# Moving four value loads behind a later head's rows, and their casts into the next unit, in a fused clustered-attention and gated feed-forward kernel

## The chip, the cores and the metric

The kernel runs on one core of one Trainium2 chip. The metric is device time in microseconds of one execution; the median of several executions is given. Beside it stands the profile of one execution: its own time, and its span, which is the time from its first to its last profiled instruction.

## The reference

Attention over 4 batches of 8 heads, 768 tokens each, head width 64. Each query and each key is assigned to the nearest of 16 centroids of its head, and a query sees only the keys of its own cluster. The result, as 3072 tokens of 512 features, goes through an RMS norm and a gated feed-forward network with 1536 hidden features.

```python
q_assign = np.argmax(np.einsum('bhsd,hcd->bhsc', q_n, c_n), axis=-1)   # q_n, k_n, c_n: normed
k_assign = np.argmax(np.einsum('bhsd,hcd->bhsc', k_n, c_n), axis=-1)
mask = q_assign[:, :, :, None] == k_assign[:, :, None, :]
scores = np.where(mask, scale * np.matmul(q, k.transpose(0, 1, 3, 2)), -1e9)
attn = softmax(scores)                              # over the keys
x = (attn @ v).transpose(0, 2, 1, 3).reshape(3072, 512)
xn = x / np.sqrt(np.mean(x * x, -1, keepdims=True) + 1e-6) * rms_g
g = xn @ w_gate
out = (g * sigmoid(g) * (xn @ w_val)) @ w_out
```

Inputs and output are float32; the kernel multiplies in bfloat16.

## The kernel before

**Units and groups.** The 32 heads (numbered 0 to 31 over batches and heads) are loaded and prepared in 8 groups of four (`group_work`); group 4 is heads 16 to 19, group 5 heads 20 to 23. The attention itself goes in 8 units, `u` = 0 to 7: unit `u` is half of the queries of batch `u // 2`, over all 8 heads of that batch. So "third unit" is `u` = 2 and "fourth unit" is `u` = 3. Groups 4 and 5 are batch 2 and are first used in the fifth unit, `u` = 4.

**Preparing a head.** SyncE's queue loads its query and key rows (`load`, L84; four transfers of 48 KB for each of the two from head 13 on) and its values (`load_v`, L103; one transfer of 192 KB). VectorE transposes the rows (`trans`, L213; L218 in the profile), GpSimd (POOL) casts them to bfloat16 into `qext` and `kext` (`cast`, L241). GpSimd also casts the values into `vbf` (`vcast`, L244). Cluster products on TensorE (L255) and comparisons on VectorE give a one-hot row of the cluster of each token, and GpSimd's queue places these by DMA under the transposed rows (`place`, L298). `vbf`, `qext` and `kext` have four buffers each, taken by group number modulo 4; the loaded values have eight buffers, and the loaded rows six.

**One unit.** For each head, TensorE computes the scores (L349), ScalarE takes the exponential (L353), and TensorE multiplies with the values one head later (`pv`, L367). Between these stands the work of earlier units: the feed-forward products of the unit before (L447, with the gate's nonlinearity on ScalarE and two products on VectorE, L468 to L473), and the output products of the one before that (L485), copied by ScalarE (L488) and stored by SyncE's queue (L489).

**From attention to feed-forward.** `rms` (L406) norms a unit's rows on VectorE (L412), and, from the second unit on, a DMA transpose issued from SyncE's queue (L417) makes `xnT`, which the gate and value products of L447 read. In the trace this transpose for the second unit's rows stands at the start of the third unit, and so on.

**What sets the order.** It is written by hand: every engine runs its instructions in program order, and the queue of an engine issues its DMAs in program order. `attention` (L690) walks over the heads of a unit and takes pieces of work from the list `fill`, each with a weight in us of TensorE work, so that they spread evenly; pieces of weight 0.0 follow the piece before them at once. In the loop at the end (L711 on) the list for a unit is: the rest of the earlier unit's feed-forward products; `rms`; then loads of query and key rows (the heads in `LATE`, L58); then output products interleaved with the rows of a new group; then feed-forward products interleaved with that group's cluster work. Group 3 is prepared in the second unit, group 4 in the third, group 5 in the fourth.

**The function that the change touches.** In `group_work`, `others(n)` runs once for each head `n` of a group, between its query cast and its key cast: it casts the head's values, loads those of head `n + 4` (`AV` = 4), and loads the rows of head `n + 6`, where these are not in `LATE`. So values of 16 to 19 are loaded during group 3's preparation, and cast during group 4's.

Of the kernel before, what the change touches and what calls it, by code (L numbers as in the profile page):

```python
# [22 lines left out]
def kernel(  # L23
# [21 lines left out]
    HG = 4  # L45
# [11 lines left out]
    AV = 4  # L57
    LATE = {2: (18, 19, 20, 21), 3: (23, 24, 25), 4: (28, 29)}  # L58
# [21 lines left out]
    def src(a, n):  # L80
        b, h = divmod(n, H)
        return a[b, h].rearrange("(p t) d -> p t d", t=ST)

    def load(n, part, on=None):  # L84
        if n not in staged:
            staged[n] = stage.tile([P, 2, ST, D], F32, tag="qk", name="qk")
        if n < BH:
            (on or nc.sync).dma_start(out=staged[n][:, part], in_=src((q, k)[part], n))
            return

        to = staged[n][:, part].rearrange("p t d -> p (t d)").rearrange("p (i r d) -> p i r d", i=HT, d=32)
        of = (q, k)[part][n // H, n % H].rearrange("(r p i e) (c d) -> e c p i r d", p=32, i=HT, e=2, d=32)
        for e in range(2):
            for c in range(2):
                r = 32 * (2 * e + c)
                nc.sync.dma_start(out=to[r:r + 32], in_=of[e, c])

    def load_qk(n):
        if n < B * H:
            load(n, 0)  # L100
            load(n, 1)

    def load_v(n, vq=None):  # L103
        if n >= B * H:
            return
        stagedv[n] = stage.tile([P, ST, D], F32, tag="vs", name="vs", bufs=NV)
        (vq or nc.sync).dma_start(out=stagedv[n], in_=src(v, n))
# [99 lines left out]
    def load_o(c):  # L207
        nc.gpsimd.dma_start(out=wo[:, c:c + 4], in_=moe_w_out[c * P:(c + 4) * P].rearrange("(c p) f -> p c f", p=P))
# [4 lines left out]
    def trans(g, h, part, on=None):  # L213
        if (g, h // 2) not in qkT:
            qkT[g, h // 2] = qk32.tile([P, 2, 2, UQ], F32, tag="qkT", name="qkT")
        qk = staged[g * HG + h]
        if g * HG + h >= BH:
            nc.vector.transpose(qkT[g, h // 2][:, h % 2, part], qk[:, part].rearrange("p t d -> p (t d)"))  # L218
            return
        ps = ps_g.tile([P, UQ], F32, tag="gen", name="tq")  # L220
        for i in range(HT):
            nc.tensor.transpose(ps[:, i * P:(i + 1) * P], qk[:, part, 2 * i:2 * i + 2].rearrange("p t d -> p (t d)"),  # L222
                                ident_f)
        to, by = qkT[g, h // 2][:, h % 2, part], 1.0 / ZS if part and g < BG else 1.0
        if on is nc.vector:
            nc.vector.tensor_scalar_mul(to, ps, by)  # L226
        else:
            nc.scalar.activation(to, ps, ACT.Copy, scale=by)  # L228
# [5 lines left out]
    def cast(on, g, h, part, es=(0, 1)):  # L234
        for e in es:
            to = cols((kext if part else qext)[g % 4][:D, h], g, e)
            of = qkT[g, h // 2][e * D:(e + 1) * D, h % 2, part]
            if on is nc.scalar:
                nc.scalar.copy(to, of)
            else:  # L240
                on.tensor_copy(to, of)  # L241

    def vcast(n):
        nc.gpsimd.tensor_copy(vbf[n // HG % 4][:, n % HG, :, :D], stagedv[n])  # L244
# [24 lines left out]
    def cluster_steps(g, m):  # L269

        of = {}

        def products():
            of["cl"] = cluster_products(g, [(h, m) for h in range(HG)])

        def most():
            of["mx"] = largest(of["cl"])

        def same():
            of["ohT"] = asg.tile([P, UQ], BF16, tag="ohT", name="ohT", bufs=2)  # L280
            compare(of["ohT"].rearrange("p (b e c) -> p b e c", e=2, c=NC), of["cl"], of["mx"])

        def back():
            put[g, m] = asg.tile([P, UQ], BF16, tag="oh", name="oh", bufs=3)
            if m and g >= BG:
                nc.vector.tensor_scalar_mul(of["ohT"], of["ohT"], ZS)
            nc.vector.transpose(put[g, m], of["ohT"])  # L287

        return [products, most, same, back]
# [3 lines left out]
    def place(on, g, m, es=(0, 1)):  # L293

        ext = (kext if m else qext)[g % 4]
        for h in range(HG):
            for e in es:
                on.dma_start(out=ext[D:D + NC, h, e * UQ:(e + 1) * UQ],  # L298
                             in_=put[g, m][32 * h + e * NC:32 * h + (e + 1) * NC])
# [205 lines left out]
    def group_work(g):  # L505

        t, c = [], []
        for h in range(HG):
            n = g * HG + h
            w = 0.0 if n >= BH else 0.3  # L510
            t += [(w, lambda h=h: trans(g, h, 0)), (w, lambda h=h: trans(g, h, 1))]

            def others(n=n):
                vcast(n)
                load_v(n + AV)
                if n == 15:
                    load(18, 0)
                if not any(n + NQ in x for x in LATE.values()):
                    load_qk(n + NQ)

            def both(h=h, f=others):
                cast(nc.gpsimd, g, h, 0)
                f()
                cast(nc.gpsimd if g * HG + h >= BH else nc.vector, g, h, 1, (0,))
            if g == 2:
                c.append((0.0, (lambda: None) if h else loads))
            else:
                c += [(0.0, both), (0.0, lambda h=h: cast(nc.gpsimd if g * HG + h >= BH else nc.vector, g, h, 1, (1,)))]
        a = []

        def values():
            place(nc.gpsimd, g, 0, (0,))
            for n in range(H, H + HG):
                vcast(n)
            load_v(14)
            load_v(15)
            load_qk(16)
            load_qk(17)

        for m in range(2):  # L540
            a += [(0.0 if i else 0.7, f) for i, f in enumerate(cluster_steps(g, m))]
            if g == 3:
                a.append((0.0, lambda m=m: place(nc.gpsimd, g, m)))
            elif g == 2:
                a += [(0.0, lambda: place(nc.gpsimd, g, 1)), (0.0, lambda: place(nc.gpsimd, g, 0, (1,))),
                      (0.0, lambda: load_o(0)), (0.0, lambda: load_o(4))] if m else [(0.0, values)]
        if g > 2:
            a[:1] = [(1.4, lambda f=(a[0][1], a.pop(5 if g == 3 else 4)[1]): [x() for x in f])]
        if g > 3:
            a.append((0.0, lambda: [place(nc.gpsimd, g, m) for m in range(2)]))  # L550
        return t, c, a
# [159 lines left out]
    for u in range(1, NU):  # L711
        ffn, o, g = ffn_work(u - 1), out_work(u - 2) if u > 1 else [], u + 2
        if u == 1:
            ffn[:2] = [(2 * 0.64, lambda: gv_first(0)), (0.0, lambda: None)]
            t, c, a = group_work(2)
            t3, c3, a3 = group_work(3)
            n = LEAD - 4
            w3 = weave(t3[n:], c3)
            prep = c + a + w3[:4] + [(0.0, lambda: load_o(8))] + w3[4:] + a3[:5]
            idle = const.tile([P, 1], BF16)  # L720

            def norm():
                rms(0)
                nc.gpsimd.tensor_copy(idle, xn[0][:, CC - 1, HT - 1, P - 1:])
                for h in range(HG):
                    casts(pool_, H + h, K0, Q0, K1, Q1)

            hooks = {(1, 0, 0): late[6], (1, 0, 1): lambda: (late[7](), norm())}
            hooks.update({(1, *divmod(2 + i, HT)): t3[i][1] for i in range(n)})
            hooks[1, *divmod(LEAD - 1, HT)] = lambda: xtrans_all(0)  # L730
            fill = spread(ffn[:CUT], prep)
            attention([(1, h) for h in range(H)], fill, LEAD, hooks)
        else:
            fill = ffn_work(u - 2)[CUT:]
            fill = fill[:1] + spread(fill[1:], [(0.0, f) for _, f in (a3[5:] if u == 2 else rest)])
            fill.append((0.0, lambda u=u: rms(u - 1)))
            rows, clusters = group(g)
            fill += [(0.0, lambda n=n: load(18, 1) if n == 18 else load_qk(n)) for n in LATE.get(u, ())]
            n, m = {2: (8, 4), 3: (12, 4)}.get(u, (len(rows), len(clusters)))
            fill += spread(o, rows[:n]) + spread(ffn[:CUT], [(0.0, f) for _, f in rows[n:]] + clusters[:m])  # L740
            rest = clusters[m:]
            attention([(u, h) for h in range(H)], fill, 1 if g < NG else 0, ahead=1)
# [42 lines left out]
```

## Time and profile before

| | |
|---|---|
| Median of three runs | 324.44 us (324.14 to 324.93) |
| The profiled execution's own time | 323.21 us |
| Its span | 321.4 us |
| Granted TensorE clock | 1.00 |
| TensorE busy with matmuls | 315.2 us |
| ScalarE, VectorE, GpSimd busy | 229.4, 216.2, 136.3 us |
| Value loads (L107) | 32, of 192 KB, median 4.0 us from issue to landing |
| Value casts (L244) | 32, median 510 ns |
| DMA transposes (L417) | 7 |

A row of the profile names the line, the engine and the operation, then what is written and read ("vbf<-vs" writes `vbf` from `vs`), the shape, and how many instructions stand together. PE is TensorE, PEld its weight loads, DVE VectorE, ACT ScalarE, POOL GpSimd, SP SyncE, and "SPq" the DMA queue of SyncE. In rows by time, the first number is the start and the second the duration, in us from the start of the span; in square brackets stands how long the engine was idle before it, and what ended that. The time of a DMA row is that of its issue; from issue to landing is told apart.

### The profile page before, as it was taken

What the parts mean: (1) busy time and instruction counts of PE and PEld (TensorE: products, weight loads), DVE (VectorE), ACT (ScalarE), POOL (GpSimd) and SP (SyncE); (2) the same over time, 40 slices, a digit from 0 to 9 for tenths busy, and PEclk for the clock granted to TensorE, in tenths of its full rate; (3) what the DMA queues carried; (4) which work ended last, traced back from release to release, by engine and by line L of the source; (5) the groups of instructions that cost most, each with busy time, mean ns of one, the idle gap of its engine ahead of it and who ended that gap; (6) DMA issues with size and microseconds to landing.
All of it is one profiled execution on the core that took longest, in us unless ns stands there. A gap on an engine that the chain in (4) does not pass through costs nothing.

```text
span 321.4 us, 7751 instructions
## 1 busy us (share of the span) xinstructions
PE 315.2 (98%) x2831; PEld 190.0 (59%) x2845; DVE 216.2 (67%) x501; ACT 229.4 (71%) x421; POOL 136.3 (42%) x277
## 2 busy tenths in 40 slices
PE   7999999999999999999999999999999999999996
PEld 3656656565656556565566655665566656654654
DVE  6999789886678857779587676876265535681430
ACT  5999878876768767777678766786778867863322
POOL 5999499898734483047917065440000000000000
PEclk9999999999999999999999999999999999999999
DMA  7999996998446654566456340000500040005002
GB/s 252 366 225 223 168 180 128 229 163 189 81 73 129 174 91 76 115 133 158 73 92 149 110 114 35 11 17 1 150 0 2 2 114 35 0 2 146 4 1 99
DMA packets 91639, 34.64 MB, mean 108 GB/s; under 512 B 75600, under 2 KB 88528, under 8 KB 91600
## 3 DMA queue, kind: packets, MB, share of 16 engines
q1 hardware_dynamic: 84544, 27.84, 36.6%
q0 software_dynamic: 6768, 5.90, 10.3%
q8 instruction: 22, 0.36, 0.5%
q10 hardware_dynamic: 288, 0.39, 0.4%
q14 instruction: 17, 0.14, 0.1%
HBM read 28.61 MB, written 6.29 MB: 109 GB/s over the span
## 4 chain that ended last, share of the span: by engine, by line
PE 93%; ACT 3%; DMA 1%; POOL 1%; issue 0%; DVE 0%; ACTq 0%
PE gate L447 20%; PE val L447 19%; PE s L349 19%; PE o L485 18%; PE acc L367 11%; PE sc L255 3%; ACT pT L353 2%; PE tq L222 2%; ACT qkT L228 1%; DMA boot<-in_centroids_dram 1%; PE o L496 1%; PE sc L321 1%; ACT L185 0%; POOL vbf L244 0%; PE tx L429 0%
## 5 line engine op out<-in xcount | busy, mean ns | idle before, releaser
L353 ACT ACTIVATE pT<-s 128x768 bf16<-128x768 f32 x192 | 155.0, 815 | 36.7 <-PE s L349 34.9
L349 PE MATMUL s<-qext,kext 80*128 80x384 bf16 x384 | 94.8, 327 | 0.4 <-ACT pT L353 0.3
L447 PE MATMUL gate<-xnT,wg 128*128 128x384 bf16 x384 | 78.6, 326 | 0.1
L447 PE MATMUL val<-xnT,wv 128*128 128x384 bf16 x384 | 78.4, 326 | 0.0
L469 DVE SCALAR_TENSOR_TENSOR th<-th,gate 128x384 f32<-128x384 f32 x81 | 44.5, 550 | 33.3 <-ACT th L468 33.3
L485 PE MATMUL o<-wo,gvT 128*128 128x512 bf16 x262 | 66.0, 378 | 0.8
L349 PEld LDWEIGHTS <-kext 80*128 80x128 bf16 x384 | 36.3, 98 | 33.5 <-issue 6.3
L468 ACT ACTIVATE th<-gate 128x384 f32<-128x384 f32 x81 | 39.7, 490 | 17.6 <-PE gate L447 17.6
L473 DVE SCALAR_TENSOR_TENSOR gvT<-th,val 128x384 bf16<-128x384 f32 x81 | 44.4, 549 | 8.7 <-PE val L447 3.5
L447 PEld LDWEIGHTS <-wg 128*128 128x128 bf16 x384 | 36.2, 97 | 23.3 <-issue 0.3
L367 PEld LDWEIGHTS <-pT 128*128 128x128 bf16 x1152 | 43.3, 97 | 9.6 <-DVE x L374 0.9
L447 PEld LDWEIGHTS <-wv 128*128 128x128 bf16 x384 | 35.7, 97 | 22.3 <-issue 0.2
L367 PE MATMUL acc<-vbf,pT 128*128 128x65 bf16 x1152 | 45.7, 193 | 0.3 <-ACT pT L353 0.3
L241 POOL CAST qext<-qkT 64x384 bf16<-64x384 f32 x64 | 34.5, 546 | 17.9 <-DVE qkT L218 9.6
L485 PEld LDWEIGHTS <-gvT 128*128 128x128 bf16 x276 | 26.0, 97 | 26.1 <-issue 0.2
L298 POOL DMA_DIRECT2D qext<-oh x48 | 23.0, 488 | 35.0 <-DVE oh L287 35.0
L241 POOL CAST kext<-qkT 64x384 bf16<-64x384 f32 x62 | 33.0, 532 | 4.6 <-DVE qkT L226 2.5
L298 POOL DMA_DIRECT2D kext<-oh x48 | 23.1, 488 | 13.3 <-DVE oh L287 11.8
L488 ACT COPY o_sb<-o 128x512 f32<-128x512 f32 x23 | 13.5, 586 | 18.6 <-PE o L485 18.6
L372 DVE RECIPROCAL inv<-acc 128x6 f32<-128x6 f32 x32 | 6.0, 187 | 25.6 <-PE acc L367 25.2
L218 DVE STREAM_TRANSPOSE qkT<-qk 128x384 f32<-128x384 f32 x38 | 19.5, 552 | 0.0
L374 DVE TENSOR_TENSOR x<-acc,inv 128x384 f32<-128x384 f32 x32 | 17.8, 558 | 1.1
(79 smaller groups left out, 218.6 us busy)
## 6 DMA issues: line engine op xcount, KB each, us to landing
vs<-in_v_dram SPq DMA_DIRECT2D x32, 192.0 KB, 4.0
out_dram<-o_sb SPq DMA_DIRECT2D x23, 256.0 KB, 2.5
qk<-in_q_dram SPq DMA_DIRECT2D x76, 48.0 KB, 2.9
qk<-in_k_dram SPq DMA_DIRECT2D x76, 48.0 KB, 2.5
qk<-in_q_dram SPq DMA_DIRECT2D x13, 192.0 KB, 4.5
qk<-in_k_dram SPq DMA_DIRECT2D x11, 192.0 KB, 4.6
wg<-in_moe_w_gate_dram POOLq DMA_DIRECT2D x2, 768.0 KB, 6.9
wv<-in_moe_w_val_dram POOLq DMA_DIRECT2D x2, 768.0 KB, 11.1
```

The source lines that it names most:

```text
L218: nc.vector.transpose(qkT[g, h // 2][:, h % 2, part], qk[:, part].rearrange("p t d -> p (t d)"))
L241: on.tensor_copy(to, of)
L298: on.dma_start(out=ext[D:D + NC, h, e * UQ:(e + 1) * UQ], in_=put[g, m][32 * h + e * NC:32 * h + (e + 1) * NC])
L349: nc.tensor.matmul(ps[:, j, :w] if nt == HT else flat[:, j * w:(j + 1) * w], lhsT=cols(kext[g % 4][:KR, hh], g, kc // HT, kc % HT * P, (kc ...
L353: nc.scalar.activation(pT[u, h][:, n * i:n * i + n, :w], of, ACT.Exp, bias=-scale * ZS, scale=scale if g >= BG else scale * ZS)
L367: nc.tensor.matmul(acc[:, h % 2, t], lhsT=pT[u, h][:, kc, t * P:(t + 1) * P], rhs=vbf[g % 4][:, hh, kc % HT * 2 + kc // HT], start=kc == 0 ...
L374: nc.vector.tensor_tensor(dst, acc[:, :, :nt, :D], inv[:, :, :nt].unsqueeze(3).broadcast_to([P, 2, nt, D]), op=ALU.mult)
L447: nc.tensor.matmul(ps, lhsT=(wv if val else wg)[:, c, f * P:(f + 1) * P], rhs=xnT[u][:, c], start=c == 0, stop=c == CC - 1)
L468: nc.scalar.activation(th, ps, ACT.Tanh, scale=0.5)
L469: nc.vector.scalar_tensor_tensor(th, th, 1.0, ps, op0=ALU.add, op1=ALU.mult)
L473: nc.vector.scalar_tensor_tensor(gvT[u][:, f, :n], gates[u], 0.5, ps, op0=ALU.mult, op1=ALU.mult)
L485: nc.tensor.matmul(outs[u], lhsT=gvT[u][:, f, t * P:(t + 1) * P], rhs=wo[:, f], start=f == 0, stop=f == FC - 1)
```

## The change

Of the heads 16 to 19 the values are loaded and cast elsewhere. `others(n)` no longer loads them (for `n` = 12 to 15, in the second unit), and no longer casts them for `n` = 16 to 19 (third unit); it casts them in the fourth unit, for `n` = 20 to 23, each ahead of the cast of head `n`. The four loads are issued in the third unit, behind the rows of head 19 and ahead of those of heads 20 and 21. In the program's order on SyncE's queue, four loads move from a place ahead of head 18's query rows (and so ahead of the first DMA transpose) to one behind head 19's key rows. On GpSimd, four casts move. TensorE, VectorE and ScalarE keep their instructions and their order.

```diff
             def others(n=n):
-                vcast(n)
-                load_v(n + AV)
+                if n // HG == 5:
+                    vcast(n - HG)
+                if n // HG != 4:
+                    vcast(n)
+                if n // HG != 3:
+                    load_v(n + AV)
                 if n == 15:
                     load(18, 0)
                 if not any(n + NQ in x for x in LATE.values()):
@@
             rows, clusters = group(g)
-            fill += [(0.0, lambda n=n: load(18, 1) if n == 18 else load_qk(n)) for n in LATE.get(u, ())]
+            if u == 2:
+                fill += [(0.0, lambda: (load(18, 1), load_qk(19)))]
+                fill += [(0.0, lambda n=n: load_v(n)) for n in range(16, 20)]
+            fill += [(0.0, lambda n=n: load_qk(n)) for n in LATE.get(u, ()) if n > 19]
             n, m = {2: (8, 4), 3: (12, 4)}.get(u, (len(rows), len(clusters)))
```

## The prediction

> **What bounds the kernel.** I read the page's busy times first, then the chain that ended last.
>
> ```profile
> span 321.4 us, 7751 instructions
> PE 315.2 (98%) x2831; PEld 190.0 (59%) x2845; DVE 216.2 (67%) x501; ACT 229.4 (71%) x421; POOL 136.3 (42%) x277
> PE 93%; ACT 3%; DMA 1%; POOL 1%; issue 0%; DVE 0%; ACTq 0%
> ```
>
> TensorE carries the chain: 93% of the span, and neither POOL nor a load of values stands in it for more than 1%. The Trainium skill warns (Perfetto Trace Analysis, Identifying the Most-Contended Engine) that busy matmul time is a poor measure, since matmuls are pipelined. So I did not stop at 98%, but asked in the stages that the change touches whether TensorE lost time there at all. The busy times by stretch, in us of the stretch (columns: PE, PEld, DVE, ACT, POOL, clock, DMA share, GB/s):
>
> ```profile
> 75.00:82.00 7.00, 6.94 (x67) 3.98 (x66) 2.57 (x7) 4.65 (x8) 5.48 (x13) 1.00 0.79 163
> 82.00:90.00 8.00, 8.00 (x66) 4.99 (x65) 6.30 (x14) 5.48 (x10) 4.61 (x10) 1.00 0.47 73
> 112.00:120.00 8.00, 7.94 (x73) 4.59 (x72) 4.39 (x11) 5.43 (x9) 6.74 (x15) 1.00 0.51 90
> 120.00:145.00 25.00, 24.95 (x233) 15.46 (x232) 18.87 (x38) 18.82 (x39) 7.09 (x15) 1.00 0.54 106
> ```
>
> These are pieces of the third unit (about 70 to 107 us) and of the fourth (107 to 144). TensorE is idle for 0.06, 0.00, 0.06 and 0.05 us in them. No more than that can be won there in this execution, and anything I make late must first use up some slack before it costs.
>
> Next, SyncE's queue in the order of time, since the change reorders it. A row is the start of the first issue, the time until the last has been issued, and how many issues.
>
> ```profile
> 71.74 1.98 SPq L107 DMA_DIRECT2D vs<-in_v_dram  x4
> 73.81 3.46 SPq L96 DMA_DIRECT2D qk<-in_q_dram  x4
> 77.45 1.57 SPq L417 DMA_TRANSPOSE xnT<-xn  x1
> 79.08 2.95 SPq L96 DMA_DIRECT2D qk<-in_k_dram  x4
> 82.07 2.62 SPq L96 DMA_DIRECT2D qk<-in_q_dram  x4
> 84.74 2.63 SPq L96 DMA_DIRECT2D qk<-in_k_dram  x4
> ```
>
> The four value loads (heads 16 to 19), the query rows of head 18, the transpose of the third unit's normed rows (xnT), the key rows of head 18, and head 19. They follow each other without a gap: the queue is the limit here, not what it waits for. The transpose's input is written by VectorE at 72.92 + 2.08 = 75.00, yet the transpose issues at 77.45, so it stands 2.4 us in the queue. What needs it is the next gate product on TensorE:
>
> ```profile
> 80.02 1.03 PE L485 MATMUL o<-wo,gvT 128*128 128x512 bf16 x4
> 80.88 0.49 PE L349 MATMUL s<-qext,kext 80*128 80x384 bf16 x2
> 81.21 0.71 PE L367 MATMUL acc<-vbf,pT 128*128 128x65 bf16 x18
> 81.75 0.81 PE L447 MATMUL gate<-xnT,wg 128*128 128x384 bf16 x4
> ```
>
> The list of DMA issues has 4.2 us from issue to landing for this transpose, so it lands at about 81.65, and the gate starts at 81.75: just in time. Did it wait? The same place of the fourth unit answers: there the output product starts at 117.18 and the gate at 118.92, 1.74 apart, and the transpose had landed at 112.34 + 3.8 = 116.14, long before. Here they are 1.73 apart. So nothing was lost, but with 0.1 us to spare.
>
> **What the Trainium skill says.** DMA: Bandwidth & Descriptors (Anatomy of one DMA) says that a semaphore wait happens on the issuing sequencer before dispatch; so whatever is ahead in SyncE's queue delays all behind it. The rows above agree: the ready transpose waited for eight issues. Perfetto Trace Analysis (DMA Instruction — HWDGE) says that the profiled time of such a DMA is the issue and not the movement of data; hence I use issue-to-landing times (4.2 us beside a row of 1.57). SBUF — State Buffer (Who interferes with whom) says that a VectorE operation with two SBUF inputs, or in a two-port mode, locks out a POOL operation that reads SBUF, and the other way round; this matters for moved casts and is weighed below.
>
> **The change, part by part.** Nothing is added or removed: four loads and four casts change their places. The order of instructions on TensorE, VectorE and ScalarE stays as it is.
>
> 1. *Four loads of values leave the place ahead of head 18's rows.* They took 73.81 - 71.74 = 2.07 us of SyncE's queue. Head 18's query rows can start at 71.74 and end at about 75.2 (with the same 3.46), and the transpose follows at max(75.0 + a tenth or two for the semaphore, 75.3), thus at about 75.4 instead of 77.45. With 4.2 us it lands at 79.6; the margin to the gate at 81.75 grows from 0.1 to about 2.1 us. Head 18's keys and head 19 come 2.07 earlier as well. Their margins before were: keys of 18, last issue about 81.3 plus 2.4 to land = 83.7, VectorE's transpose at 85.28; keys of 19, last issue 86.7 plus 2.4 = 89.1, transpose at 89.97. No wait stood there; gain 0.
>
> 2. *The same loads are put behind head 19.* That ends at 87.37 - 2.07 = 85.3, and four issues of the same kind take 2.07 again, so head 20's rows start where they did, at 87.4. From there on the queue is as before: sum 0. Bounds: one issue of this kind took 327 to 1918 ns (median 376), so four lie between 1.3 and 7.7 us, or -0.7 to +5.7 against the 1.98 of their own row. What is queued behind: heads 20 and 21, three output stores, the loads of values 20 to 23, and the fourth unit's transpose. The queue is through at 106.85 + 0.91 = 107.76, and that transpose waits for its input until 112.34: 4.58 us of cover. It lands at 116.14, the gate needs it at 118.92: 2.78 more. Only beyond 7.36 us does TensorE wait; +5.7 costs nothing. The stores' buffers are no nearer: the first store issues at 98.51 and lands about 2.5 later, and ScalarE rewrites its buffer at 110.88. I take 0.
>
> 3. *Four casts leave the third unit.* POOL's casts there come with waits of 0.96 and 2.14 us for rows that are not yet there, so 4 x 0.51 = 2.04 us becomes more idle time on an engine that nobody waits for. 0.
>
> 4. *Four casts go into the fourth unit*, one ahead of each value cast of heads 20 to 23.
>
> ```profile
> 112.82 1.05 POOL L241 CAST qext<-qkT 64x384 bf16<-64x384 f32 x2 [0.70 <-DVE inv L372]
> 113.93 0.51 POOL L244 CAST vbf<-vs 128x384 bf16<-128x384 f32 x1
> 122.14 1.05 POOL L241 CAST qext<-qkT 64x384 bf16<-64x384 f32 x2 [1.31 <-PE val L447]
> 123.25 0.51 POOL L244 CAST vbf<-vs 128x384 bf16<-128x384 f32 x1
> 123.83 1.06 POOL L241 CAST kext<-qkT 64x384 bf16<-64x384 f32 x2
> 137.55 3.81 POOL L298 DMA_DIRECT2D qext<-oh  x8 [12.66 <-DVE oh L287]
> ```
>
> POOL's burst runs from 112.82 to 124.89. Three of the four casts (1.53 us) first eat the 1.31 us gap before 122.14; the end moves to 125.6, or with the slowest such cast (877 ns, so 4 x 0.88 = 3.5 us) to at most 128.4. Then comes an idle stretch of 12.66 us, ended by VectorE at 137.55. What waits for POOL meanwhile: head 20's values are wanted by no one before the fifth unit, which begins past 144 us, and so are the moved ones (heads 16 to 19); VectorE's row transposes of this unit overwrite buffers that earlier bursts have read. 0. The lock on SBUF's port: on VectorE between 112.8 and 128 there are only row transposes (one input) and products with an input in PSUM; the operation with two SBUF inputs (L412, normed rows) ends at 112.19, the next (L267) starts at 135.09. So no collision with up to 15 us of room.
>
> 5. *Two waits of new order.* The load of head 24's values reuses head 16's buffer and so waits for its cast; that was done in the third unit, now at about 114.4. The load issues at 132.29, 18 us later. Each cast waits for its load: landed by 85.3 + 2.1 + 5 = 92.4, the cast at 113.9. 0.
>
> The sum over the profiled execution: 0, so its span stays at 321.4 us and its own time at 323.21. The median of the three timed runs is 324.44, 1.23 us above the profiled execution; against it the sum is also 0: **324.4 us**.
>
> **Rivals.** *The transpose was late in the timed runs (faster).* The margin of 0.1 us is of one execution, and it is a race between SyncE's queue, which follows the DMAs, and TensorE, which doesn't. The timed runs are 324.14 to 324.93, all above the profiled 323.21. If all of the 1.23 us came from this wait, the change would bring 323.2; half of it 323.8. For it: of the seven such transposes the other six waited for their input; this one alone stands in a backlog. Against: a difference between a profiled and a timed execution needs no such cause, and this trace has no wait at that gate.
>
> *SyncE's queue gives back more than it gained (slower).* The value loads now stand just ahead of heads 20 and 21 and the stores. If each issue waits for an earlier DMA to land, the fourth unit's transpose comes late. It decides from 7.36 us of extra queue time; beyond, each us costs one. At twice the slowest issue seen (4 x 3.84 = 15.3, +13.4) the transpose would miss by 6.0 us: 330.5. A miss just large enough to be seen (8.3 us extra) would give 325.4. Against it: not even the slowest row reaches the point.
>
> *The change doesn't do what it says.* Were the transpose held by its input or a buffer and not by the queue, it would stay near 77.4. VectorE's end at 75.00 speaks against; the time would be the same, 324.4.
>
> **How the numbers follow.** About 0.3% (1.0 us) is what a measurement of this kernel can tell from no change. Hidden everywhere: 0.66, at 324.4, spread by the runs' own 0.3 to 0.5 either way (323.9 to 325.0). The late transpose: 0.25, evenly over gains of 0 to 1.23 us, of which a fifth is over 1.0; with a little for a larger effect than the profile lets me see I put 0.09 on faster. The queue: 0.06, slower. No move of the transpose: 0.03, same. So faster 0.09, same 0.85, slower 0.06. The range takes the hidden case with its spread and most of the late transpose: 323.5 to 325.0; it leaves out the largest gains and the slow rival.
>
> **What would show it.** In the changed kernel's trace the transpose in the third unit issues near 75.4 (step 1), the four value loads near 85.3 and head 20's rows at 87.4 (step 2), POOL's burst in the fourth unit ends at about 125.6 before an idle stretch of some 12 us (step 4), and TensorE is idle for no more than 0.1 us in the stretches above. A gate that waits at 118.9, or a fourth transpose after 115, would show the slow rival; a span of 321.4 with timed runs down by a microsecond would show the late transpose. I am wrong if TensorE's own durations shift, or if a wait that the trace puts on nobody bounds a timed run.

## The result

The changed kernel takes 323.2 us (median of six runs, 322.72 to 323.45), beside 324.69 us (324.14 to 325.05) for the kernel before. The ratio is 0.9953, with a 95% interval of 0.9939 to 0.9966: 1.5 us faster. I had forecast no change, 324.4 us. The direction that I gave 9% came, at the place that I had named in a rival.

The profiles alone would mislead. The page of the kernel after:

```profile
span 321.5 us, 7755 instructions
PE 316.0 (98%) x2845; PEld 190.0 (59%) x2845; DVE 217.4 (68%) x501; ACT 229.4 (71%) x421; POOL 135.8 (42%) x277
```

Its span is 321.5 us where that of before was 321.4; its profiled execution took 323.24 us (323.21 before). The profile of after is a typical execution of its kernel; that of before lay 0.9 us below the fastest of the kernel's six timed runs. Of the 150 timed executions of the kernel before that stand beside the experiments below, a single one was faster than its profiled one (323.15 us; their medians are 324.49 to 324.68). So the gain is about the difference between a typical and a lucky execution of the kernel before, and the two traces hardly differ.

SyncE's queue in the kernel after (start of the first issue, time of issuing, how many):

```profile
73.39 2.97 SPq L96 DMA_DIRECT2D qk<-in_q_dram  x4
76.53 1.41 SPq L417 DMA_TRANSPOSE xnT<-xn  x1
77.99 3.33 SPq L96 DMA_DIRECT2D qk<-in_k_dram  x4
81.36 2.63 SPq L96 DMA_DIRECT2D qk<-in_q_dram  x4
84.03 2.62 SPq L96 DMA_DIRECT2D qk<-in_k_dram  x4
86.76 1.98 SPq L107 DMA_DIRECT2D vs<-in_v_dram  x4
88.79 2.61 SPq L96 DMA_DIRECT2D qk<-in_q_dram  x4
```

The value loads are gone from ahead of the transpose, which issues at 76.53, and head 20's rows begin at 88.79. TensorE around the third unit's gate, and POOL at the end of its burst in the fourth unit:

```profile
80.06 1.03 PE L485 MATMUL o<-wo,gvT 128*128 128x512 bf16 x4
81.26 0.71 PE L367 MATMUL acc<-vbf,pT 128*128 128x65 bf16 x18
81.80 0.81 PE L447 MATMUL gate<-xnT,wg 128*128 128x384 bf16 x4
```

```profile
124.27 1.07 POOL L241 CAST kext<-qkT 64x384 bf16<-64x384 f32 x2
137.59 0.49 POOL L298 DMA_DIRECT2D qext<-oh  x1 [12.25 <-DVE oh L287]
```

The gate starts 1.74 us after the last output product ahead of it: no wait, as in the lucky execution of before. POOL's burst ends at 125.34 with 12.25 us of idle time behind it.

### The profile page after: what moved, and what is told of

It is laid out like the page before. It is cut to its first block, busy times and chain, and to the rows that moved or that the text cites. A ratio compares the mean times of both kernels' runs of the same rounds, so it can differ in the third digit from the quotient of the medians.

```text
span 321.5 us, 7755 instructions
## 1 busy us (share of the span) xinstructions
PE 316.0 (98%) x2845; PEld 190.0 (59%) x2845; DVE 217.4 (68%) x501; ACT 229.4 (71%) x421; POOL 135.8 (42%) x277
## 4 chain that ended last, share of the span: by engine, by line
PE 93%; ACT 3%; DVE 2%; DMA 1%; issue 0%; DVEq 0%; ACTq 0%
PE gate L447 20%; PE val L447 19%; PE s L349 19%; PE o L485 19%; PE acc L367 11%; PE sc L255 3%; ACT pT L353 1%; DMA boot<-in_centroids_dram 1%; PE tq L222 1%; PE o L496 1%; ACT qkT L228 1%; DVE scT L324 1%; PE sc L321 1%; ACT L185 0%; DVE pads L328 0%
## 5 line engine op out<-in xcount | busy, mean ns | idle before, releaser
L447 PE MATMUL gate<-xnT,wg 128*128 128x384 bf16 x384 | 78.6, 326 | 0.1
L485 PE MATMUL o<-wo,gvT 128*128 128x512 bf16 x276 | 67.7, 378 | 0.0
L367 PEld LDWEIGHTS <-pT 128*128 128x128 bf16 x1152 | 43.4, 97 | 9.4 <-DVE x L374 0.8
L367 PE MATMUL acc<-vbf,pT 128*128 128x65 bf16 x1152 | 45.7, 193 | 0.3 <-ACT pT L353 0.3
```

What stands on the lines that cost most here:

```text
L367: nc.tensor.matmul(acc[:, h % 2, t], lhsT=pT[u, h][:, kc, t * P:(t + 1) * P], rhs=vbf[g % 4][:, hh, kc % HT * 2 + kc // HT], start=kc == 0 ...
L447: nc.tensor.matmul(ps, lhsT=(wv if val else wg)[:, c, f * P:(f + 1) * P], rhs=xnT[u][:, c], start=c == 0, stop=c == CC - 1)
L485: nc.tensor.matmul(outs[u], lhsT=gvT[u][:, f, t * P:(t + 1) * P], rhs=wo[:, f], start=f == 0, stop=f == FC - 1)
```

## The experiments

Theory T: in most executions of the kernel before, the transpose lands after its gate is due, and TensorE waits. R: the rows of heads 18 and 19 are late, and VectorE holds the gate products. P: POOL's casts in the third unit hold something. The experiments moved instructions only; none leaves out part of the computation. They were run in three groups, each on one chip beside runs of the kernel before: first the kernel before again, only the casts, rows first and the transpose ahead; then half, all ahead, the changed kernel again and the transpose at the head; then only the loads, and second runs of three of these.

To measure waits independently of where an execution started, I use a ruler in the chain of work: the eight output products in a row of each unit. In both first traces they start 37.17 us apart from the third to the fourth unit (before: 75.19 and 112.36; after: 75.24 and 112.41). What a trace shows above 37.17 was lost between.

**The kernel before again**, unchanged, for the trace of another execution.

> The kernel before, unchanged, for the trace of another of its executions. Theory T (in the timed runs the third unit's transpose lands after its gate is due): ratio 1.000, timed runs 324.1 to 325.1; if the profiled execution is a typical one (span about 322.5 to 323, a microsecond above 321.4), the transpose lands at 82.5 to 83.5 and TensorE is idle ahead of the gate at about 81.8 by as much as the span is longer. Rival R (rows of heads 18 and 19 land late and hold VectorE's row transposes, and the gate products behind them): the idle time stands after 84 us, with VectorE's L218 waiting for a transfer of qk. Rival P (GpSimd's four casts in the third unit hold something): no wait on TensorE near 82, and a wait that POOL ends.

Measured: 324.64 us, ratio 1.000 (0.9985 to 1.0015); profiled execution 324.24 us, span 322.5. First its queue, then TensorE in the order of time:

```profile
73.18 2.91 SPq L107 DMA_DIRECT2D vs<-in_v_dram  x4
76.18 2.59 SPq L96 DMA_DIRECT2D qk<-in_q_dram  x4
78.94 1.57 SPq L417 DMA_TRANSPOSE xnT<-xn  x1
```

```profile
81.56 0.71 PE L367 MATMUL acc<-vbf,pT 128*128 128x65 bf16 x18
82.80 0.81 PE L447 MATMUL gate<-xnT,wg 128*128 128x384 bf16 x4 [0.52 <-DMA xnT<-xn]
```

And the chain of work, which in this execution runs through the transpose and on into the fourth unit's output products:

```profile
75.55 1.73 PE o L485 x8
78.94 3.81 DMA xnT<-xn
113.39 1.73 PE o L485 x8
```

The transpose issues 1.5 us later than in the first trace, lands at 78.94 + 3.81 = 82.75, and the gate starts at 82.80. The ruler reads 37.84: 0.67 us lost. (The bracket names less, 0.52, because it counts from the recorded end of the products with the values (L367), 0.71 behind their start. In the first trace the gate starts 0.54 behind that start: the rows of pipelined products overlap.) This is the wait that the first trace of the same kernel lacked. Nearly all the rest of the longer span, 0.36 us, stood before 75 us (75.55 against 75.19).

**Only the casts move.**

```diff
 # the changed kernel, with
-                if n // HG != 3:
-                    load_v(n + AV)
+                load_v(n + AV)
 # and without the four loads behind head 19
-                fill += [(0.0, lambda n=n: load_v(n)) for n in range(16, 20)]
```

> Only the casts of heads 16 to 19 move to the fourth unit; their loads stay ahead of head 18's query rows, so SyncE's queue is that of the kernel before. T: 324.7, ratio 1.000 (within 0.002), since the transpose issues where it did. R: 1.000 too, since the rows come as before. P: the whole gain, 323.2, ratio 0.995.

Measured: 324.68 us, ratio 1.0001 (0.9986 to 1.0015). P falls. Its trace waits too:

```profile
79.27 1.57 SPq L417 DMA_TRANSPOSE xnT<-xn  x1
```

```profile
80.88 0.71 PE L367 MATMUL acc<-vbf,pT 128*128 128x65 bf16 x18
83.12 0.81 PE L447 MATMUL gate<-xnT,wg 128*128 128x384 bf16 x4 [1.53 <-DMA xnT<-xn]
```

This execution was earlier than the others at 75 us (74.86), and simply waited longer: the ruler reads 113.71 - 74.86 = 38.85: 1.68 us lost.

**Only the loads move**: the changed kernel with the casts back in the third unit.

```diff
 # the changed kernel, with
-                if n // HG == 5:
-                    vcast(n - HG)
-                if n // HG != 4:
-                    vcast(n)
+                vcast(n)
```

> The changed kernel with the four casts back in the third unit: only the loads are moved. GpSimd then waits for head 16's values (landing near 91) in the middle of its burst, which ends near 97 to 98 instead of 92.4; its next work is at 100.65. T: the transpose issues as in the changed kernel, so the same gain, ratio 0.995 to 0.9965. P: no gain or a loss, since the casts are in the third unit and later than ever: 1.000 or more.

Measured: 323.15 us, ratio 0.9947 (0.9928 to 0.9966): the whole gain. POOL waits in the middle of its burst, and it costs nothing:

```profile
90.30 0.50 POOL L244 CAST vbf<-vs 128x384 bf16<-128x384 f32 x1 [10.71 <-DMA vs<-in_v_dram]
100.97 3.81 POOL L298 DMA_DIRECT2D qext<-oh  x8 [0.88 <-DVE oh L287]
```

So the moved casts bring nothing by themselves; what they do is to save POOL that wait of 10.71 us, which leaves 0.88 us of room ahead of its next work.

**The rows first, the transpose behind them.**

```diff
 # the changed kernel, with
                 if n == 15:
-                    load(18, 0)
+                    load_qk(18)
-                fill += [(0.0, lambda: (load(18, 1), load_qk(19)))]
+                fill += [(0.0, lambda: load_qk(19))]
```

> The changed kernel, but head 18's key rows too are issued ahead of the transpose: loads of values out of the way, casts in the fourth unit, rows of 18 and 19 at least as early as in the changed kernel, the transpose behind four more issues (2.6 to 3 us) and so some 0.5 to 1 us later than in the kernel before. T: the gain is gone, 324.7 to 325.9, ratio 1.000 to 1.004. R: 323.2, ratio 0.995. P: 323.2, ratio 0.995.

Measured: 325.43 us, ratio 1.0024 (1.0006 to 1.0043). Loads and casts are where the change puts them, the rows are early, and still the gain is gone: R and P fall. The transpose issues at 79.52, and the gate waits (0.73 us named, 0.88 by the ruler):

```profile
79.52 1.58 SPq L417 DMA_TRANSPOSE xnT<-xn  x1
```

```profile
83.39 0.81 PE L447 MATMUL gate<-xnT,wg 128*128 128x384 bf16 x4 [0.73 <-DMA xnT<-xn]
```

**The transpose ahead of head 18's query rows, all else as before.**

```diff
 # the kernel before, with
-                if n == 15:
-                    load(18, 0)
-            fill += [(0.0, lambda n=n: load(18, 1) if n == 18 else load_qk(n)) for n in LATE.get(u, ())]
+            fill += [(0.0, lambda n=n: load_qk(n)) for n in LATE.get(u, ())]
```

> The kernel before, but head 18's query rows are issued behind the transpose, the four value loads still ahead of both and the casts where they were. The transpose issues about 2 us earlier (near 75.3), the rows of heads 18 and 19 no earlier, rather up to 1 us later. T: the whole gain, 323.2, ratio 0.995. R: 324.7 or slower, ratio 1.000 to 1.003. P: 324.7, ratio 1.000.

Measured: 324.32 us, ratio 0.9987 (0.9972 to 1.0002). Less than T expected: its trace has no wait at the gate (ruler 37.17), but the timed runs show only a quarter of the gain. So I ran it again beside the changed kernel:

> The kernel before with head 18's query rows behind the transpose, beside the changed kernel this time, since alone it gave 324.32 (ratio 0.9987) where T expected 323.2. T, with a margin that is too small in part of the executions (the value loads ahead still wait for earlier transfers, so the transpose issues between 75.5 and 78): ratio between that of the kernel before and the changed kernel's, 0.996 to 0.999. T with a margin as large as in the changed kernel: equal to it within 0.0012. R: 1.000.

Measured: 323.69 us, ratio 0.9972 (0.9957 to 0.9986); the changed kernel beside it 0.9960 (0.9942 to 0.9979). The intervals overlap, so this pair doesn't tell the two apart; together with the first run it is likely that only part of the gain is there. The new trace shows two ways in which it can be lost. The transpose issues early, at 76.51, but directly behind four transfers of 192 KB it takes 5.8 us to land, so at 82.31, where the gate starts at 82.45. And a different wait stands ahead of it:

```profile
80.35 0.50 PE L349 MATMUL s<-qext,kext 80*128 80x384 bf16 x2 [0.33 <-DMA kext<-oh]
```

Scores wait for the one-hot rows that POOL's queue places in the same microseconds. By the rows in time, the eight output products start at 75.20 and 112.89, so 0.52 us were lost. POOL is as late with them as in the first trace of the changed kernel, which shows no wait (the query side begins at 72.67, there at 72.68); but of the key side's placings issued between 76 and 78.6 us the median takes 4.4 us to land, and 3.5 there. It may be that the value loads in flight hold up what TensorE needs by more than their place in SyncE's queue; I did not test it apart. I saw this second wait in one execution only. In the two traces with the old queue that lose time, all of it is lost at the gate.

**Half of the loads ahead.**

```diff
 # the changed kernel, with
-                if n // HG != 3:
+                if n not in (14, 15):
                     load_v(n + AV)
-                fill += [(0.0, lambda n=n: load_v(n)) for n in range(16, 20)]
+                fill += [(0.0, lambda n=n: load_v(n)) for n in (18, 19)]
```

> The changed kernel with two of the four value loads (heads 16 and 17) back ahead of head 18's query rows. The transpose issues about 1 us later than in the changed kernel. T: about half of the gain left, 323.6 to 324.2, ratio 0.997 to 0.9985.

Measured: 323.89 us, ratio 0.9981 (0.9969 to 0.9994): half of the gain, as expected (the changed kernel on the same chip: 0.9964). Its profiled execution, at 324.65 us, is one of its slow ones and waits 1.43 us by the ruler, so that trace is not typical of it.

**Head 18's rows and the values, all ahead of the transpose.**

```diff
 # the kernel before, with
                 if n == 15:
-                    load(18, 0)
+                    load_qk(18)
-            fill += [(0.0, lambda n=n: load(18, 1) if n == 18 else load_qk(n)) for n in LATE.get(u, ())]
+            fill += [(0.0, lambda n=n: load_qk(n)) for n in LATE.get(u, ()) if n != 18]
```

> The kernel before with head 18's key rows issued ahead of the transpose too: the four value loads and all of head 18's rows stand ahead of it, with no transfer added. The transpose issues 2.6 to 3 us later than in the kernel before, near 81.5, and lands near 85.5; the rows of head 18 come earlier. T: its whole delay is paid by TensorE at the gate, a wait of 3 to 4 us, 327.0 to 327.7, ratio 1.007 to 1.009; the fourth unit's output products start 40 to 41 us after the third's instead of 37.17. R: 324.0 to 324.7, ratio 0.998 to 1.000.

Measured: 328.77 us, ratio 1.0122 (1.0108 to 1.0137): T's direction, and 1.1 us more than its range. The transpose issues at 82.18 and lands 3.86 later, and the gate waits 4.08 us, as expected. What is beyond that is TensorE's clock. The rows by time, and then the stretches (TensorE's busy time and instructions first, the granted clock third from the end):

```profile
81.29 0.71 PE L367 MATMUL acc<-vbf,pT 128*128 128x65 bf16 x18
86.08 1.44 PE L447 MATMUL gate<-xnT,wg 128*128 128x384 bf16 x4 [4.08 <-DMA xnT<-xn]
```

```profile
84.00:86.00 2.00, 0.00 (x0) 0.00 (x0) 0.00 (x0) 0.00 (x0) 0.01 (x1) 0.50 0.92 167
88.00:90.00 2.00, 2.00 (x8) 0.96 (x7) 1.60 (x3) 0.57 (x2) 0.00 (x0) 0.50 0.47 74
90.00:92.00 2.00, 2.00 (x12) 1.08 (x11) 0.72 (x2) 0.92 (x3) 1.51 (x3) 0.82 0.46 72
```

The clock fell to 0.50 during the wait and stayed there until past 90 us; four gate products took 1.44 us instead of 0.81. The ruler reads 118.94 - 75.27 = 43.67: 6.5 us lost. Of these, 4.25 lie between the time at which the gate would have followed (81.29 + 0.54 = 81.83) and its start. The other 2.25 are the slow clock: from the start of this gate to the next products of L367 TensorE takes 6.49 us, and 4.24 in the first trace of the kernel before. The profiled execution was the slowest of the four (329.79 us, mean clock 0.990); the others, at 328.00 to 328.78, show a mean clock of 0.995, so they seem to have lost less to it.

**The changed kernel again, and with the transpose at the very head**, on two chips.

```diff
 # the changed kernel, with
-                if n == 15:
-                    load(18, 0)
-                fill += [(0.0, lambda: (load(18, 1), load_qk(19)))]
+                fill += [(0.0, lambda: (load_qk(18), load_qk(19)))]
```

> The changed kernel again, as the measure for the runs beside it. T: ratio 0.995, no wait of TensorE at the third unit's gate, and the eight output products of the fourth unit start 37.17 us after those of the third, as in both traces without a wait. R and P make no other forecast here.

> The changed kernel with head 18's query rows too behind the transpose: the transpose is the first issue after head 17's rows, so it waits for its input alone (about 75.3) and lands near 79.5, over 2 us ahead of its gate. T: as the changed kernel or a little better, if some of its timed runs still wait: 322.9 to 323.2, ratio 0.994 to 0.995. R: rows of 18 some 1 to 2 us later than in the changed kernel, so 323.2 to 324.5.

> The changed kernel as the measure on this chip. T: 0.995 to 0.9965.

> The changed kernel with head 18's query rows behind the transpose as well, to see whether it beats the changed kernel beyond noise. T: no TensorE wait at the gate in either; up to 0.001 below the changed kernel if some of its executions still wait there, else equal.

Measured: the changed kernel 323.45 us, 0.9964 (0.9952 to 0.9976), and 323.33 us, 0.9960 (0.9942 to 0.9979). With the transpose at the head 322.96 us, 0.9954 (0.9942 to 0.9966), and 323.49 us, 0.9948 (0.9932 to 0.9965). In the traces with the transpose at the head it issues at 75.15 and 76.01, as soon as nothing but its input holds it, and lands at about 79.7 and 80.6, 1.8 and 1.6 us ahead of the gate. In the two traces of the changed kernel it lands at about 81.3 and 82.2, and the gate starts at 81.66 and 82.22. The second of these is a close one:

```profile
81.61 0.71 PE L367 MATMUL acc<-vbf,pT 128*128 128x65 bf16 x18
82.22 0.81 PE L447 MATMUL gate<-xnT,wg 128*128 128x384 bf16 x4
```

The gate starts 0.61 us behind the start of the products with the values (L367) instead of 0.54 or 0.55, and the ruler reads 37.23: 0.06 us lost, with the transpose landing at that very time. So the change has not taken the transpose out of the race; it has moved it to the winning side, by tenths of a microsecond. The other three rulers are 37.16, 37.17 and 37.17.

The transpose at the head is not told apart from the changed kernel: the intervals overlap, and of its two medians one is below the changed kernel's and one above. (The recorded ratio is not always the quotient of the medians: 323.49 beside 324.60 would be 0.9966.) So little is left to win at this gate.

All fourteen traces together, in us (the lucky one of before first; "landed" is issue plus the time to landing as listed):

| Execution | Issued | Landed | Gate starts | Lost by the ruler |
|---|---|---|---|---|
| before, first trace | 77.45 | 81.65 | 81.75 | 0.00 |
| before, again | 78.94 | 82.75 | 82.80 | 0.67 |
| only the casts moved | 79.27 | 83.08 | 83.12 | 1.68 |
| rows first | 79.52 | 83.35 | 83.39 | 0.88 |
| half | 78.53 | 83.17 | 83.21 | 1.43 |
| all ahead | 82.18 | 86.04 | 86.08 | 6.50 |
| transpose ahead of head 18's rows | 76.81 | 81.4 | 82.33 | 0.00 |
| the same, second run | 76.51 | 82.3 | 82.45 | 0.52 |
| only the loads moved | 77.32 | 81.6 | 81.74 | 0.00 |
| changed kernel | 76.53 | 81.2 | 81.80 | 0.00 |
| changed kernel, second run | 76.72 | 81.3 | 81.66 | 0.00 |
| changed kernel, third run | 77.97 | 82.2 | 82.22 | 0.06 |
| transpose at the head | 75.15 | 79.7 | 81.48 | 0.00 |
| the same, second run | 76.01 | 80.6 | 82.17 | 0.00 |

Wherever the trace names the transpose as what ended the wait, the gate starts 0.04 or 0.05 us behind the landing.

The spans show that nothing else differs behind the third unit. From the fourth unit's eight output products to the end of the span, every one of the fourteen traces takes 209.0 or 209.1 us. So two traces differ only by when the third unit's products start (74.9 to 75.9 us) and by what the ruler shows as lost. The start shows no dependence on where the value loads stand: 74.86 to 75.55 with the queue of the kernel before, 75.10 to 75.59 in the changed kernel. This allows an estimate for the executions that left no trace. A timed execution of the kernel before has a span of about 322.8 us (median). Less 209.1 and 37.2 that is 76.5, so with starts as in its traces some 0.9 to 1.6 us are lost. The changed kernel's 321.5 leaves 75.2: about nothing is lost.

## Why the prediction was wrong

**The step that failed** is the last line of the sum: "against it the sum is also 0". Steps 1 to 5 were sums over one execution, and I carried their zero over to the timed runs, in which step 1 is worth about a microsecond, although the profiled execution stood 1.23 us below their median. For this kernel that execution is an unusual one: of three traces with its queue (two of the kernel before, one with only the casts moved) two wait at the gate, 0.67 and 1.68 us. The mean of these two is 1.2 us (0.8 for all three), beside a gain of 1.0 to 1.5 us in the three comparisons with the changed kernel; three traces are too few for more than the size. With a margin that I had put at 0.1 us, and a queue without a gap ahead of it, I should have asked how much the queue's own time varies; in three traces with this queue the transpose issued between 77.45 and 79.27, 1.8 us apart, while TensorE at 75 us varied by 0.7.

**Step 1**, the four loads leaving: right in kind. The "gain 0" was the lucky execution's, and that this execution was the one profiled was chance. The loads' time in the queue was mis-sized too: 2.07 us in the first trace, 2.91 and 2.75 in the two others plus a tenth to the next issue. And the new margin is not 2.1 us: the transpose issued at 76.53, not at 75.4, since the queue was then ready only at 73.39, and it took 4.7 us to land instead of 4.2. The margin in the traced execution is 0.57 us; in the second trace it is some 0.3, with only the loads moved some 0.1, and in the third trace there is none. Nor did the ready transpose wait for eight issues, as the prediction says: when its input was written, at 75.00, the four value loads were out (71.74 + 1.98), and it waited for what was left of head 18's query rows, which they had pushed back.

**Step 2**, the loads behind head 19: right that nothing is lost. Head 20's rows came at 88.79, 1.4 later than I wrote, again from the later start of the whole queue, and the fourth unit's transpose still issued at 112.39, when its input was ready.

**Steps 3 and 4**, POOL: right. Moving the casts alone is worth 1.0001; the burst's end was 125.34 (125.6 forecast), with 12.25 us of idle time behind it (some 12). POOL's two waits in the third unit, 0.96 and 2.14 us, were not for rows that had not come: VectorE transposed these rows only behind other work of its own, at 84.27 and 89.03, just ahead of the casts. That changes nothing in the sum. No run tests the lock on SBUF's port.

**Step 5**: right. In the first trace of the changed kernel neither the casts of the moved values nor the load of head 24's values waits.

**The rivals.** The late transpose was the true case; its sign, a span of 321.4 with timed runs down by a microsecond, is what came (321.5), and at its own values of 323.2 to 323.8 it named the result. That the number fits so well is partly luck: the gain of 1.5 us is above the 1.23 that the rival allowed, and on the other two chips it was 1.0 and 1.3. My argument against it, that "this trace has no wait at that gate", was an argument about one execution. Its chance of 0.25 and a fifth of that for a clear gain were too low: the 1.23 us between the profiled execution and the median had no other cause that I could name, and should have weighed more for this race on TensorE. The slow rival did not come; the experiment with all loads ahead shows what it looks like when a transpose is late by microseconds.

**What stays open.** Why SyncE's queue is done with head 17's rows between 71.7 and 74.8 us from execution to execution was not tested. Nor is it known why the transpose ahead of head 18's rows alone brings only part of the gain: its two traces lose nothing and 0.52 us, the second at the one-hot rows, and whether value loads in flight cause that was not tested. Transposes issued earlier took longer to land (3.8 or 3.9 us from 78.9 on, 4.2 to 4.7 before 78 in the changed kernel), which gives part of an earlier issue back. Why is open too.

## What to carry to other kernels

When a transfer lands a tenth of a microsecond ahead of its use, and a backlogged queue sets its time, one trace without a wait doesn't show that there is none: compare the profiled execution with the timed ones, and if it is faster than all of them, look for the narrow races first. The same holds for the trace after the change: a race won by tenths of a microsecond can still be lost. Put the transfer that the bound engine waits for ahead of bulk loads whose use is far away. A ruler between two landmarks of the bound engine tells a wait in between from a different start, and makes traces comparable.

## What the runs showed of the hardware

In the execution with all loads ahead, a wait of about 4.2 us cost 6.5 us: TensorE's granted clock fell to 0.50 in it and was still there nearly 4 us after work had resumed (0.50 from 88 to 90 us, work from 86.08), while waits of up to 1.7 us left it at 1.00. The Trainium skill (TensorE: Matmul & The Clock Gate, Why this matters for your kernels) advises against idle gaps of TensorE over some 3 us for this reason; these runs agree as far as they go (1.7 us did no harm, 4.2 us did, and nothing between was run). And the time from issue to landing of one and the same DMA transpose differs by half: 3.8 to 4.2 us in the three traces with the queue of the kernel before, 4.2 to 4.7 in those of the changed kernel, 4.6 and 5.8 directly behind the four value loads. Whether the transfers in flight set it was not tested.
